# One decode step with its gradients on one core: weight and gradient transfers moved from POOL's DMA queue to ScalarE's ring

## The chip, the cores and the metric

The kernel runs on one core of a Trainium2 chip. The time is device microseconds (us) of one execution; several executions of the unchanged kernel were timed, and one more was recorded by the hardware profiler. PE is the matrix engine, DVE the vector engine, ACT (ScalarE) the activation engine, POOL (GpSimd) the general one, SP (SyncE) an engine that here only issues transfers. A transfer (DMA) is issued by an instruction in an engine's in-order queue and carried by the core's 16 DMA engines.

## The reference

A gated mix of two branches for one token of width 640, and the gradients of everything but one input:

```python
x = A_x                                            # 1 x 1 x 640, bf16
g = sigmoid((x * gate_w).sum(-1))
q = (x @ wq) as 32 heads of 128                    # wq 640 x 4096
p = softmax(q . k_cache * 128**-0.5)               # k_cache, v_cache: 32 x 4096 x 128
a = (p . v_cache) @ wo                             # wo 4096 x 640
h = B_x @ w1 + b1                                  # w1 640 x 1728
b = (h * tanh(softplus(h))) @ w2                   # w2 1728 x 640
out = g * a + (1 - g) * b
# and, for grad_out: d A_x, d k_cache, d v_cache, d wq, d wo, d w1, d b1, d w2, d gate_w
```

Each of K, V, dK and dV is 32 MiB, so 128 MiB of the traffic belong to the caches and their gradients.

## The kernel before, in words

Work goes head by head (32 heads, `h`), in groups of four (`g`, eight groups; `hh` is the head's place in its group). The order of all instructions is written out by hand.

One head: PE transposes V in four blocks (`v_tr`, L448) and ACT copies each block out (L449); the softmax of the head's scores is finished meanwhile (`softmax`: `mx`, `negM`, `e_bf`). DVE makes the previous head's dK (`dk_out`, L511, tile `o_sb`), and SP stores it (L524). `dP` multiplies by the transposed V; the next head's K is transposed and copied (`k_tr`); `probs` finishes p and ds; `dv_out` makes dV. Then `scores(h + 1)` (L454, whose maxima end in ACT's `dgm`, L476), and `dq_o` (L534), the products with V and K themselves. After that SP issues the loads of K for head h + 4 and V for head h + 3: K has four buffers, V three, and `o_sb` four.

Between these steps the code puts the work by groups. For the next group (g + 1): `g_do` (DVE, reads wo) in the third and fourth heads, `g_qcol` (reads wq) in the third, `g_q` in the fourth. For the previous group (g − 1): the gradient of x through wq (`f_dx`), and the gradients of wq and wo, which are written over the weights in place: `f_dwq` on DVE (L317), `f_dwo` on ACT (L323), then the stores `f_dwq_st` (L320) and `f_dwo_st` (L326). A group's wq is 640 rows of 1,024 bytes and its wo 512 rows of 1,280 bytes, 640 KiB each; each has three buffers.

Loads of these weights (`load_wq` L116, `load_wo` L120): group 0 from POOL's queue at the start, groups 1 and 2 from SP's, and the others from POOL's, in the second head of the group two before, after that head's stores. All stores of them are in POOL's queue.

The MLP's work is handed out in small steps in every head from the third on (`mlp_some`, `dw2_some`). Its hidden row is computed in five pieces on one partition, copied to SBUF by ACT (L348) and spread over partitions by five small transfers (L350, L352); two row buffers take turns. Its gradients dw1 and dw2 are written over w1 and w2; their stores stand at L703 to L706, in head 28 of 0 to 31.

The last head is written out after the loop, with the last group's gradients in parts and the small rows of the outputs at the end (L773 to L775). The framework adds the waits on semaphores; an engine runs its own list in order, whatever the others do.

Of the kernel before, what the change touches and what calls it, by code (L numbers as in the profile page):

```python
# [16 lines left out]
def kernel(  # L17
# [24 lines left out]
    nc = tc.nc  # L42
    P = 128
    _, H, Sk, Dh = A_k_cache.shape
    D = A_x.shape[-1]
    F = B_w1.shape[1]
    assert Dh == P and Sk == 32 * P and D % P == 0 and H % 4 == 0 and H >= 16
    J = Sk // P
    RC = D // P
    G = 4  # L50
    NG = H // G
    GD = G * Dh
    FR = F // P
    FM = FR * P
    FT = F - FM
    FCN = FR + 1
# [14 lines left out]
    dwq_v = out_4.rearrange("(rc r) c -> r rc c", r=P)  # L71
    wo_v = A_wo.rearrange("(h d) n -> d h n", d=P)
    dwo_v = out_5.rearrange("(h d) n -> d h n", d=P)
    w1_v = B_w1.rearrange("(rc r) f -> r rc f", r=P)
    dw1_v = out_6.rearrange("(rc r) f -> r rc f", r=P)
    w2_v = B_w2[0:FM, :].rearrange("(p fc) n -> p fc n", p=P)
    dw2_v = out_8[0:FM, :].rearrange("(p fc) n -> p fc n", p=P)
    b1_v = B_b1[0:FM].rearrange("(p fc) -> p fc", p=P)
    b1_t = B_b1[FM:F].rearrange("(p o) -> p o", o=1)
# [6 lines left out]
    out1_rows = out_1.rearrange("a b (c p) -> (a b c) p", p=P)  # L86
# [15 lines left out]
    kts, vts, wqs, wos = {}, {}, {}, {}  # L102
# [6 lines left out]
    def load_v(h):  # L109
        if h < H:  # L110
            vts[h] = kv_in.tile([P, J, Dh], BF16, name="Vn", tag="Vn", bufs=VBUFS)
            nc.sync.dma_start(vts[h][:], Vv[h])

    def load_wq(g, eng):
        wqs[g] = wts.tile([P, RC, GD], BF16, name="wq_g", tag="wq_g")
        eng.dma_start(wqs[g][:], wq_v[:, :, g * GD:(g + 1) * GD])  # L116

    def load_wo(g, eng):
        wos[g] = wts.tile([P, G, D], BF16, name="wo_g", tag="wo_g")
        eng.dma_start(wos[g][:], wo_v[:, g * G:(g + 1) * G, :])  # L120
# [7 lines left out]
    kts[0] = kv_in.tile([P, J, Dh], BF16, name="Kn", tag="Kn")  # L128
    for c in range(2):
        nc.sync.dma_start(kts[0][:, c * JH:(c + 1) * JH, :], Kv[0][:, c * JH:(c + 1) * JH, :])  # L130
    load_wq(0, nc.gpsimd)
    load_wo(0, nc.gpsimd)
    load_v(0)
    load_k(1)
    load_v(1)
# [5 lines left out]
    w1_sb = const.tile([P, RC, F], BF16, name="w1_sb")  # L141
    nc.sync.dma_start(w1_sb[:], w1_v)
    w2_sb = const.tile([P, FCN, D], BF16, name="w2_sb")
# [2 lines left out]
    nc.sync.dma_start(w2_sb[0:FT, FR, :], B_w2[FM:F, :])  # L146
    b1_sb = const.tile([P, FCN], BF16, name="b1_sb")
    nc.vector.memset(b1_sb[:], 0.0)
    nc.gpsimd.dma_start(b1_sb[:, 0:FR], b1_v)
    nc.gpsimd.dma_start(b1_sb[0:FT, FR:FCN], b1_t)  # L150

    ident_bf = const.tile([P, P], BF16, name="ident_bf")
    nc.gpsimd.memset(ident_bf[:], 0.0)
# [10 lines left out]
    def grp(shape, dt, name):  # L164
        return grp_ps.tile(shape, dt, name=name, tag="grp")
# [72 lines left out]
    def g_dobc(g):  # L238
        g_bcast(groups[g]["do_diag"], groups[g]["do_row"], 0, G)
# [11 lines left out]
    def f_bc(g, a=0, b=G):  # L251
        g_bcast(groups[g]["dq_diag"], groups[g]["dq_bc"], a, b)

    def f_aT_pe(g, a=0, b=G):
        gp = groups[g]
        gp["aT_ps"] = grp([P, RC], F32, "aT_ps")
        for c in range(RC):
            for hh in range(a, b):
                nc.tensor.matmul(gp["aT_ps"][:, c:c + 1], lhsT=wos[g][:, hh, c * P:(c + 1) * P],
                                 rhs=gp["o_bf"][:, hh:hh + 1], start=(hh == a), stop=(hh == b - 1))  # L260
# [56 lines left out]
        nc.vector.tensor_scalar(wqs[g][:, c, cs], groups[g]["dq_bc"][:, cs], x_col_f[:, c:c + 1], None, ALU.mult)  # L317

    def f_dwq_st(g):
        nc.gpsimd.dma_start(dwq_v[:, :, g * GD:(g + 1) * GD], wqs.pop(g)[:])  # L320

    def f_dwo(g, hh):
        nc.scalar.activation(wos[g][:, hh, :], da_bc[:], ACT.Copy, scale=groups[g]["dqo"][:, 1, hh:hh + 1])  # L323

    def f_dwo_st(g, a=0, b=G):
        nc.gpsimd.dma_start(dwo_v[:, g * G + a:g * G + b, :], wos[g][:, a:b, :])  # L326

    h_sb = const.tile([P, FCN], F32, name="h_sb")
    u_sb = const.tile([P, FCN], F32, name="u_sb")
# [11 lines left out]
    def m_h(i):  # L341
        n = FW if i < 4 else FT
        ps = grp([1, FW], F32, "h_ps")
        for rc in range(RC):
            nc.tensor.matmul(ps[:, 0:n], lhsT=x_col_bf[:, rc:rc + 1], rhs=w1_sb[:, rc, i * FW:i * FW + n],
                             start=(rc == 0), stop=(rc == RC - 1))
        row = dh_bc[0:1, :].bitcast(F32)[:, (i % 2) * FW:(i % 2) * FW + n]
        nc.scalar.copy(row, ps[:, 0:n])  # L348
        if i < 4:
            nc.gpsimd.dma_start(h_sb[i * P // 4:(i + 1) * P // 4, 0:FR], row)  # L350
        else:
            nc.gpsimd.dma_start(h_sb[0:FT, FR:FCN], row)  # L352

    def m_np(fc):
        return P if fc < FR else FT
# [107 lines left out]
    def v_tr(h, c):  # L463
        if c == 0:
            VT[h] = kvT.tile([P, J, P], BF16, name="VT", tag="VT")
        tr_block(vts[h], VT[h], c)
# [11 lines left out]
    def softmax(h):  # L478
        mx = s_ps.tile([P, P + 2], F32, name="mx", tag="mx")
        nc.tensor.matmul(mx[:, 0:P], lhsT=scale_f[:], rhs=dgms.pop(h)[:], start=True, stop=True)  # L480
        negM = small.tile([P, 1], F32, name="negM", tag="negM")
        nc.vector.tensor_reduce(negM[:], mx[:, 0:P], axis=AX.X, op=ALU.max, negate=True)  # L482
        es[h] = small.tile([P, J], BF16, name="e_bf", tag="e_bf")
        zds[h] = small.tile([P, 2], F32, name="zd", tag="zd")
        nc.scalar.activation(es[h][:], S_ps.pop(h)[:], ACT.Exp, bias=negM[:], scale=scale, accum_out=zds[h][:, 0:1])  # L485
        return mx

    def dP(h):
        DP_ps[h] = s_ps.tile([P, J], F32, name="DP", tag="DP")
        cols_mm(DP_ps[h][:], VT.pop(h), doz[h // G % 2][:, h % G, :])  # L490
        pj = small.tile([P, J], F32, name="pj", tag="pj")
        nc.vector.scalar_tensor_tensor(pj[:], in0=DP_ps[h][:], scalar=1.0, in1=es[h][:],
                                       op0=ALU.mult, op1=ALU.mult, accum_out=zds[h][:, 1:2])
# [32 lines left out]
    def dv_out(h):  # L526
        out_pair(h, dVv, p4s[h], groups[h // G]["do_row"])

    def dk_out(h):
        out_pair(h, dKv, ds4s[h], groups[h // G]["qs_row"])  # L530
# [92 lines left out]
    for h in range(H - 1):  # L623
        g, hh = h // G, h % G
        nx, pv = g + 1 < NG, g > 0
        v_tr(h, 0)
        v_tr(h, 1)
        mx = softmax(h)
        if h > 0:
            dk_out(h - 1)  # L630
        if hh == 0 and pv:
            g_dobc(g)
        v_tr(h, 2)
        v_tr(h, 3)
        dP(h)
        if hh == 0 and pv:
            f_bc(g - 1)
            f_aT_pe(g - 1)
        k_tr(h + 1, 0)
        k_tr(h + 1, 1)  # L640
        zd_mm(h, mx)
        if hh == 0 and pv:
            f_dx(g - 1, 0)
        if hh == 1 and pv:
            f_dx(g - 1, 3)
        if hh == 2 and nx:
            g_do(g + 1, 0)
        if hh == 3 and nx:
            g_do(g + 1, 3)
        probs(h, mx)  # L650
        k_tr(h + 1, 2)
        k_tr(h + 1, 3)
        dv_out(h)
        scores(h + 1)
        od = dq_o(h)
        load_k(h + KBUFS)
        load_v(h + VBUFS)
        dqo_red(h, od)
        budget = 0.0
        if hh == 0:  # L660
            if nx:
                g_new(g + 1)
            if pv:
                f_aT_add(g - 1)
                f_dx(g - 1, 1)
                f_dx(g - 1, 2)
                f_dwo(g - 1, 0)
                f_dwo(g - 1, 1)
            budget = 2.7
        if hh == 1:  # L670
            if pv:
                f_dx(g - 1, 4)
                for c in range(RC):
                    f_dwq(g - 1, c)
                f_dwq_st(g - 1)
                f_dwo(g - 1, 2)
                f_dwo(g - 1, 3)
                f_dwo_st(g - 1)
            if g + 2 < NG:
                load_wq(g + 2, nc.gpsimd if pv else nc.sync)  # L680
                load_wo(g + 2, nc.gpsimd if pv else nc.sync)
            budget = 1.8
        if hh == 2:
            if nx:
                g_do(g + 1, 1)
                g_do(g + 1, 2)
                g_qcol(g + 1)
            budget = 2.7
        if hh == 3:
            if nx:  # L690
                g_docol(g + 1)
                g_dodiag(g + 1)
                g_q(g + 1)
                g_qs(g + 1)
                f_new(g)
                f_diag(g)
            budget = 1.8
        if h >= 2:
            mlp_some(budget)
            dw2_some(2)  # L700
        if h == H - 4:
            assert not mq and dw2_next[0] == FCN
            nc.gpsimd.dma_start(dw1_v, w1_sb[:])  # L703
            for a, b in W2P:
                nc.gpsimd.dma_start(dw2_v[:, a:b, :], w2_sb[:, a:b, :])
            nc.gpsimd.dma_start(out_8[FM:F, :], w2_sb[0:FT, FR, :])  # L706
            nc.sync.dma_start(db1_row, dh_bc[0:1, :])

    g, h = NG - 1, H - 1
# [61 lines left out]
    fin_rows = const.tile([3 * RC, P], BF16, name="fin_rows")  # L771
    nc.scalar.copy(fin_rows[:], fin_ps[:])
    nc.scalar.dma_start(out0_rows, fin_rows[0:RC, :])  # L773
    nc.gpsimd.dma_start(out1_rows, fin_rows[RC:2 * RC, :])
    nc.scalar.dma_start(out9_rows, fin_rows[2 * RC:3 * RC, :])  # L775
    dk_out(h)

# [29 lines left out]
```

## Time and profile before

| | |
|---|---|
| median of 3 runs | 418.42 us (418.15 to 419.58) |
| profiled execution | 420.13 us, its span 418.4 us |
| busy PE, DVE, ACT, POOL | 320.5, 303.1, 216.3, 38.1 us |
| moved by DMA | 165.05 MB, mean 395 GB/s |
| of that in SP's and in POOL's queue | 141.28 MB and 22.79 MB |
| mean granted TensorE clock | 0.893 |

The span is the time from the first to the last instruction. In the profile's list of slices each digit is a fortieth of the span, busy share in tenths. In its DMA part, q1 is the hardware ring that SP uses, q10 the one that ACT uses, and q0 the queue that POOL feeds by software. A wait is told as the line that waited and what it waited for, with the total, the number of times and the longest. DMA share is the mean busy share of the 16 engines; it can read slightly over 1.

### The profile page before, as it was taken

How to read it: one execution, taken by the hardware profiler on the slowest of the kernel's cores; microseconds unless marked ns; L12 is line 12 of the kernel's file. 1: busy time of each engine (PE TensorE's matmuls, PEld its weight loads, DVE VectorE, ACT ScalarE, POOL GpSimd, SP SyncE). 2: the span in 40 equal slices, each digit the busy share in tenths (PEclk: the TensorE clock that was granted, in tenths of full speed). 3: DMA queues.
4: the chain of work that ended last, by engine and by line, in shares of the span. 5: the costliest groups of instructions: out<-in, count | busy, mean ns of one | idle time of the engine just before them, and what ended most of it. 6: DMA issues, size and time to landing. Idle time of an engine off the chain costs nothing.

```text
span 418.4 us, 15402 instructions
## 1 busy us (share of the span) xinstructions
PE 320.5 (77%) x6797; PEld 291.5 (70%) x6797; DVE 303.1 (72%) x816; ACT 216.3 (52%) x447; POOL 38.1 (9%) x61
## 2 busy tenths in 40 slices
PE   1598959888699779777987889777897888847850
PEld 1487838777679778767877778666787787747740
DVE  0536645787868987798869796888887987718681
ACT  2255434674346635455666764665445644545560
POOL 5000010001100100001104100001000040000120
PEclk9999898999789998888998898878988989959985
DMA  8999999999999999999999999999999999999956
GB/s 292 394 408 422 420 397 418 417 378 412 404 406 356 387 417 405 414 411 404 410 389 420 424 418 408 421 415 352 407 385 423 383 418 420 416 421 415 401 228 244
DMA packets 28074, 165.05 MB, mean 395 GB/s; under 512 B 3093, under 2 KB 5462, under 8 KB 12007
## 3 DMA queue, kind: packets, MB, share of 16 engines
q1 hardware_dynamic: 22402, 141.28, 83.7%
q0 software_dynamic: 5552, 22.79, 13.8%
q8 instruction: 53, 0.87, 0.8%
q14 instruction: 15, 0.11, 0.1%
q10 hardware_dynamic: 52, 0.01, 0.0%
HBM read 82.03 MB, written 82.03 MB: 392 GB/s over the span
## 4 chain that ended last, share of the span: by engine, by line
PE 39%; ACT 22%; DVE 20%; DMA 11%; issue 5%; DVEq 0%; POOL 0%; ACTq 0%; POOLq 0%
PE tr L448 16%; PE od L534 11%; ACT VT L449 8%; ACT KT L449 7%; DMA out_dram<-o_sb 6%; DVE o_sb L511 4%; DMA wo_g<-in_A_wo_dram 3%; PE S L454 3%; PE DP L454 3%; DVE junk L408 2%; PE q_ps L197 2%; DVE junk L219 2%; DVE junk L270 2%; DVE mjunk L430 2%; ACT e_bf L485 2%
## 5 line engine op out<-in xcount | busy, mean ns | idle before, releaser
L448 PE MATMUL tr<-ident_bf,Vn 128*128 128x128 bf16 x1024 | 78.8, 236 | 24.7 <-ACT VT L449 15.5
L449 ACT COPY KT<-tr 128x512 f32<-128x512 f32 x128 | 70.5, 587 | 48.7 <-PE tr L448 48.6
L448 PEld LDWEIGHTS <-Vn 128*128 128x128 bf16 x1024 | 70.4, 107 | 35.4 <-issue 25.3
L448 PE MATMUL tr<-ident_bf,Kn 128*128 128x128 bf16 x1024 | 83.5, 245 | 6.9 <-DMA Kn<-in_A_k_cache_dram 5.0
L448 PEld LDWEIGHTS <-Kn 128*128 128x128 bf16 x1024 | 76.9, 114 | 8.8 <-DMA Kn<-in_A_k_cache_dram 4.9
L449 ACT COPY VT<-tr 128x512 f32<-128x512 f32 x128 | 69.4, 586 | 23.4 <-PE tr L448 22.8
L511 DVE TENSOR_TENSOR o_sb<-qs_row,ds 128x2048 bf16<-128x2048 bf16 x64 | 78.1, 1263 | 2.9 <-DMA out_dram<-o_sb 2.9
L511 DVE TENSOR_TENSOR o_sb<-do_row,p 128x2048 bf16<-128x2048 bf16 x64 | 75.2, 1217 | 1.1 <-DMA out_dram<-o_sb 1.1
L454 PE MATMUL DP<-doz,VT 128*128 128x32 bf16 x1024 | 39.6, 179 | 27.9 <-ACT VT L449 24.1
L454 PEld LDWEIGHTS <-VT 128*128 128x128 bf16 x1024 | 33.2, 98 | 32.9 <-ACT VT L449 31.8
L454 PE MATMUL S<-qz,KT 128*128 128x32 bf16 x1024 | 36.9, 180 | 3.1 <-ACT KT L449 0.4
L476 ACT ACTIVATE dgm<-ident_bf,m 128x128 f32<-128x128 bf16 x32 | 12.9, 402 | 50.3 <-DVE m L474 50.3
L454 PEld LDWEIGHTS <-KT 128*128 128x128 bf16 x1024 | 32.4, 98 | 6.4 <-ACT KT L449 5.8
L534 PE MATMUL od<-p,Vn 128*128 128x32 bf16 x1024 | 31.5, 177 | 3.9 <-issue 3.9
L534 PE MATMUL od<-ds,Kn 128*128 128x32 bf16 x1024 | 31.2, 177 | 2.3 <-issue 2.3
L534 PEld LDWEIGHTS <-Vn 128*128 128x128 bf16 x1024 | 28.4, 96 | 4.4 <-issue 4.4
L534 PEld LDWEIGHTS <-Kn 128*128 128x128 bf16 x1024 | 28.3, 96 | 2.6 <-issue 2.6
L270 DVE SCALAR_TENSOR_TENSOR junk<-wq_g,dq_bc 128x512 bf16<-128x512 bf16 x35 | 23.5, 687 | 4.0 <-ACT dq_bc L233 4.0
L320 POOL DMA_DIRECT2D out_dram<-wq_g x8 | 7.1, 886 | 206.6 <-DVE wq_g L317 108.0
L219 DVE SCALAR_TENSOR_TENSOR junk<-wo_g,da_bc 128x640 bf16<-128x640 bf16 x32 | 25.5, 820 | 0.4 <-DMA wo_g<-in_A_wo_dram 0.4
L482 DVE TENSOR_REDUCE negM<-mx 128x1 f32<-128x128 f32 x32 | 9.2, 288 | 22.8 <-PE mx L480 22.7
L323 ACT ACTIVATE wo_g<-da_bc,dqo 128x640 bf16<-128x640 bf16 x32 | 24.5, 813 | 0.0
(157 smaller groups left out, 326.8 us busy)
## 6 DMA issues: line engine op xcount, KB each, us to landing
out_dram<-o_sb SPq DMA_DIRECT2D x62, 1024.0 KB, 10.4
Vn<-in_A_v_cache_dram SPq DMA_DIRECT2D x32, 1024.0 KB, 14.8
Kn<-in_A_k_cache_dram SPq DMA_DIRECT2D x31, 1024.0 KB, 15.5
out_dram<-wq_g POOLq DMA_DIRECT2D x8, 640.0 KB, 10.5
out_dram<-wo_g POOLq DMA_DIRECT2D x7, 640.0 KB, 14.2
wq_g<-in_A_wq_dram POOLq DMA_DIRECT2D x6, 640.0 KB, 11.7
wo_g<-in_A_wo_dram POOLq DMA_DIRECT2D x6, 640.0 KB, 12.1
w_sb<-in_B_w_dram SPq DMA_DIRECT2D x1, 2160.0 KB
```

The source lines that it names most:

```text
L197: nc.tensor.matmul(ps[:], lhsT=x_col_bf[:, rc:rc + 1].to_broadcast([P, P]), rhs=wqs[g][:, rc, :], start=(rc == 0), stop=(rc == RC - 1))
L219: nc.vector.scalar_tensor_tensor(junk[:], in0=wos[g][:, hh, :], scalar=1.0, in1=da_bc[:], op0=ALU.mult, op1=ALU.mult, accum_out=gp["do_col ...
L270: nc.vector.scalar_tensor_tensor(junk[:, cs], in0=wqs[g][:, c, cs], scalar=1.0, in1=gp["dq_bc"][:, cs], op0=ALU.mult, op1=ALU.mult, accum_ ...
L323: nc.scalar.activation(wos[g][:, hh, :], da_bc[:], ACT.Copy, scale=groups[g]["dqo"][:, 1, hh:hh + 1])
L408: nc.vector.scalar_tensor_tensor(junk[0:n, :], in0=w2_sb[0:n, fc, :], scalar=dm[0:n, fc:fc + 1], in1=db_bc[0:n, :], op0=ALU.mult, op1=ALU. ...
L448: nc.tensor.transpose(tp[:, t, :], src[:, c * TB + t, :], ident_bf[:])
L449: nc.scalar.copy(dst[:, sl, :].rearrange("p a b -> p (a b)").bitcast(F32), tp[:].rearrange("p a b -> p (a b)").bitcast(F32))
L454: nc.tensor.matmul(out, lhsT=T[:, j, :], rhs=zrow[:, J - 1 - j:2 * J - 1 - j], start=(j == 0), stop=(j == J - 1))
L476: nc.scalar.activation(dgms[h][:], ident_bf[:], ACT.Copy, scale=m32[:])
L482: nc.vector.tensor_reduce(negM[:], mx[:, 0:P], axis=AX.X, op=ALU.max, negate=True)
L511: nc.vector.tensor_tensor(dst[:, a:b, :].rearrange("p j (k t) -> p j k t", t=4), row.rearrange("p (k t) -> p k t", t=4).unsqueeze(1).to_br ...
L534: nc.tensor.matmul(out, lhsT=N[:, j, :], rhs=c4[:, 4 * j:4 * j + W], start=(j == 0), stop=(j == J - 1))
```

## The change

- Group 0's wq and wo are loaded from SP's queue, wq after the first half of head 0's K, wo after its second half.
- The other loads of wq and wo from group 2 on, all stores of their gradients but one, the two pieces of b1, the hidden row's five transfers, the stores of dw1 and dw2 and one output row are issued by ScalarE. The store of the last group's wq gradient is issued by SP.
- The weights of group g + 1 are loaded at the end of the first head of group g (from g = 1 on), where before those of g + 2 were loaded in the second head of g.
- The store of a group's wq gradient stands one head later, in the third head of the next group.

```diff
     for c in range(2):
         nc.sync.dma_start(kts[0][:, c * JH:(c + 1) * JH, :], Kv[0][:, c * JH:(c + 1) * JH, :])
-    load_wq(0, nc.gpsimd)
-    load_wo(0, nc.gpsimd)
+        (load_wo if c else load_wq)(0, nc.sync)
...
-    nc.gpsimd.dma_start(b1_sb[:, 0:FR], b1_v)
-    nc.gpsimd.dma_start(b1_sb[0:FT, FR:FCN], b1_t)
+    nc.scalar.dma_start(b1_sb[:, 0:FR], b1_v)
+    nc.scalar.dma_start(b1_sb[0:FT, FR:FCN], b1_t)
...
     def f_dwq_st(g):
-        nc.gpsimd.dma_start(dwq_v[:, :, g * GD:(g + 1) * GD], wqs.pop(g)[:])
+        (nc.sync if g == NG - 1 else nc.scalar).dma_start(dwq_v[:, :, g * GD:(g + 1) * GD], wqs.pop(g)[:])
...
     def f_dwo_st(g, a=0, b=G):
-        nc.gpsimd.dma_start(dwo_v[:, g * G + a:g * G + b, :], wos[g][:, a:b, :])
+        nc.scalar.dma_start(dwo_v[:, g * G + a:g * G + b, :], wos[g][:, a:b, :])
...
         if i < 4:
-            nc.gpsimd.dma_start(h_sb[i * P // 4:(i + 1) * P // 4, 0:FR], row)
+            nc.scalar.dma_start(h_sb[i * P // 4:(i + 1) * P // 4, 0:FR], row)
         else:
-            nc.gpsimd.dma_start(h_sb[0:FT, FR:FCN], row)
+            nc.scalar.dma_start(h_sb[0:FT, FR:FCN], row)
...
         if hh == 0:
+            if nx and pv:
+                load_wq(g + 1, nc.scalar)
+                load_wo(g + 1, nc.scalar)
             if nx:
                 g_new(g + 1)
...
                     f_dwq(g - 1, c)
-                f_dwq_st(g - 1)
                 f_dwo(g - 1, 2)
                 f_dwo(g - 1, 3)
                 f_dwo_st(g - 1)
-            if g + 2 < NG:
-                load_wq(g + 2, nc.gpsimd if pv else nc.sync)
-                load_wo(g + 2, nc.gpsimd if pv else nc.sync)
             budget = 1.8
         if hh == 2:
+            if pv:
+                f_dwq_st(g - 1)
...
         if h == H - 4:
             assert not mq and dw2_next[0] == FCN
-            nc.gpsimd.dma_start(dw1_v, w1_sb[:])
+            nc.scalar.dma_start(dw1_v, w1_sb[:])
             for a, b in W2P:
-                nc.gpsimd.dma_start(dw2_v[:, a:b, :], w2_sb[:, a:b, :])
-            nc.gpsimd.dma_start(out_8[FM:F, :], w2_sb[0:FT, FR, :])
+                nc.scalar.dma_start(dw2_v[:, a:b, :], w2_sb[:, a:b, :])
+            nc.scalar.dma_start(out_8[FM:F, :], w2_sb[0:FT, FR, :])
...
-    nc.gpsimd.dma_start(out1_rows, fin_rows[RC:2 * RC, :])
+    nc.scalar.dma_start(out1_rows, fin_rows[RC:2 * RC, :])
```

## The prediction

> **What bounds the kernel now.** I read the page first, its slices and DMA queues above all.
>
> ```profile
> PE 320.5 (77%) x6797; PEld 291.5 (70%) x6797; DVE 303.1 (72%) x816; ACT 216.3 (52%) x447; POOL 38.1 (9%) x61
> DMA  8999999999999999999999999999999999999956
> DMA packets 28074, 165.05 MB, mean 395 GB/s; under 512 B 3093, under 2 KB 5462, under 8 KB 12007
> q1 hardware_dynamic: 22402, 141.28, 83.7%
> q0 software_dynamic: 5552, 22.79, 13.8%
> PE 39%; ACT 22%; DVE 20%; DMA 11%; issue 5%; DVEq 0%; POOL 0%; ACTq 0%; POOLq 0%
> ```
>
> No engine is over 77%, POOL is not on the chain of waits, and the 16 DMA engines are full until some 20 us before the end. Two limits lie close together: a relay of PE, ACT and DVE of 11.9 us a head (a group's q_ps, the last of its four heads, starts at 69.6 and at 354.5 us, six groups apart: 285/24), and the DMA. A group moves 16 MiB of K, V and their gradients and 2.5 MiB of weights and theirs, 19.4 MB in 47.5 us, 408 GB/s. The stretches (columns: PE, PEld, DVE, ACT, POOL busy, clock, DMA share, GB/s) show how near that is to the most the DMA does:
>
> ```profile
> 18.00:24.00 6.00, 3.67 (x17) 1.99 (x17) 2.57 (x11) 1.64 (x4) 0.00 (x0) 1.00 1.05 381
> 54.00:60.00 6.00, 3.19 (x28) 1.93 (x28) 2.50 (x6) 0.87 (x2) 1.04 (x2) 1.00 1.06 388
> 150.00:156.00 6.00, 4.78 (x128) 4.39 (x124) 4.98 (x13) 1.48 (x3) 0.86 (x1) 1.00 1.02 420
> 366.00:372.00 6.00, 0.00 (x0) 0.00 (x0) 1.50 (x8) 1.84 (x3) 0.00 (x0) 0.54 1.02 421
> 396.00:402.00 6.00, 5.29 (x154) 4.90 (x152) 3.54 (x10) 4.62 (x9) 0.00 (x0) 1.00 0.36 145
> ```
>
> In the fourth row PE does nothing for 6 us: V of head 29 is late. In the last the DMA is two thirds idle, since the last heads' outputs are not made yet. The timelines and the waits say why:
>
> ```profile
> 336.89 0.86 POOL L703 DMA_DIRECT2D out_dram<-w_sb  x1
> 366.48 1.53 ACT L323 ACTIVATE wo_g<-da_bc,dqo 128x640 bf16<-128x640 bf16 x2
> 372.06 1.89 PE L448 MATMUL tr<-ident_bf,Vn 128*128 128x128 bf16 x16 [6.63 <-DMA Vn<-in_A_v_cache_dram]
> ...
> 11.95 0.69 PE L209 MATMUL qc_ps<-cols_bf,wq_g 128*128 128x1 bf16 x20 [4.99 <-DMA wq_g<-in_A_wq_dram]
> ...
> SPq L120 <- DMA vec_rows<-in_gate_w_dram: 0.4, 1, 0.4
> SPq L707 <- DMA Vn<-in_A_v_cache_dram: 3.6, 1, 3.6
> ```
>
> The 4.4 MB of dw1 and dw2, written in the code at head 28, leave at 337 us, during head 25: POOL has nothing else in its queue and runs ahead. They hold up V29. The last two rows show SP holding a transfer for an unrelated one. The instruction records name the reason: SP's and ScalarE's transfers take turns on the same eight completion semaphores, and one is issued when the earlier holder of its semaphore has landed. POOL's have eight of their own.
>
> **The change part by part**, against the profiled execution (420.13 us, span 418.4); the median, 418.42, is 1.7 lower, and I carry differences over to it.
>
> *Start.* wq and wo of group 0 shared the engines with K0, V0, K1; wq landed at 11.9 us, wo about 15.5 to 16.2. On SP between the halves of K0, wq has only 0.52 MB ahead of it: from the first bytes at 2.3 us, 1.18 MB at some 360 GB/s (GB/s is 227 to 400 over 2 to 8 us) is 5.6 us, and 1 us or so to land: 7.0. Likewise wo 9.7. From wq to the first g_do took 4.4 us, so head 0 starts 4.9 us earlier. V0 and K1, now behind 1.31 MB more, land near 11.5 and 14 and are used from 18 and 22. Cover: the prefetch; without it the gain shrinks to nothing. Bounds −4.9 to 0; I take −4.9. The two b1 transfers go onto ScalarE's ring ahead of its first copy (6.0 us), two issues of 0.3 us: hidden, unless rival 3 holds.
>
> *Issue time.* On SP a wq transfer took 0.43 us to issue, wo 0.38 (the second wo's 3.64 us was SP's ring full with 1,800 rows; ScalarE's has at most 1,152 of weights). ScalarE gets, in each of groups 1 to 6: wq and wo in the group's first head (0.81), dwo in its second (0.38), dwq in its third (0.43). In first heads, ScalarE today goes from dgm through two f_dwo (1.53) straight into the V copies, 0.9 to 1.1 us from dgm's end: nothing hides the 0.81. In second heads likewise, with f_dwo_st behind the last f_dwo. In third heads it waits 1.0 to 2.2 us there with nothing to do: 0.43 hidden. So 1.2 us × 6 = 7.2 us in the way of the copies. The chain runs through f_dwo in three of seven groups, which makes 3.1 us the floor; I take 5.1. The five h_sb transfers move with their 5 us landing (L348 waits 4.4 for one): nothing, ±2. POOL's own 0.86 and 0.77 us issues were on no chain: nothing.
>
> *Packets.* The page's counts tell how each ring cuts the rows. 2,369 packets lie between 512 B and 2 KB, and SP's two wq, two wo and the tail of w2 have 2,368 rows of 1,024 and 1,280 B: a hardware ring moves row by row. POOL's 14 wq-shaped and 14 wo-shaped transfers alone are 16,128 rows in 5,552 packets: joined by four. The packet records give 46 ns for 1,024 B, 58 for 1,280, and 159 for 4,096, 196 for 5,120. Per pair, (640 × (46 − 159/4) + 512 × (58 − 196/4))/16 = 0.54 us. The first two stretches above, with such pairs, lose (418−381)/418 × 6 = 0.53 and 0.43 us. Twelve pairs before head 28's end: 6.5 us, if stores cost what loads do (none is in the trace on a hardware ring: from 0 to 10). Against that stands that 3.5 MB of dw1 and dw2 no longer pass by then, 8.4 us at 415 GB/s. So the DMA has 1.9 us less to do by that point, and I take 0, with +6.5 as the bound, if heads 1 to 24 are held by the DMA.
>
> A rule speaks differently here: in the Trainium skill, DMA: Bandwidth & Descriptors, section Specifications, transfers reach line rate from 512 B; these rows would then cost nothing extra, and the sum would be the same with a bound of 0. The 46 ns row decides. The same page (Issuing engines are not separate DMA queues) says that all issuers use the same engines and that only issue time is saved; by that rule the move off POOL brings nothing at all.
>
> *Weights one group ahead.* They are issued at the end of a group's first head and wanted by g_do in its third, some 20 us on; such pairs on POOL's ring landed in 10 to 14 us (counting its completion packets). Covered by 6 us; nothing. Without cover DVE waits, some 2 us a group.
>
> *Tail.* f_dwo of head 28 ends at 368.0 us; then ScalarE issues dw1, dw2 (three) and the remainder: 5 × 0.44 = 2.2. V29 is in time now, so its copies start at 370.2, not 373.19: −3.0. But the eight semaphores: the fifth of the burst needs V30 landed, the fourth K31, issued at 352.9 to 356.2 us. Landings of V took 10 to 17 us with no dw stores about, so V30 lands at 366 to 374: a wait of 0 to 6 us with the copies of V29 queued behind it on ScalarE, PE behind them; I take 3. From there 46 us of relay remain, and the DMA has 17.5 MB left: 42.2 us at 415 GB/s and 1.1 for two pairs. It fits, so the idle stretch fills at no gain. Last, dwq of group 7 goes ahead of SP's last outputs and more transfers share the eight semaphores: 0 to 2, I take 1.
>
> *Mid-run waits.* dwo's issue needs K of the head before landed: 12 us after that issue; K landed after 9 to 14, and the new weight loads add up to 1.31 MB/410 = 3.2. So between none and 5 us; over six groups I take 1 us in all, the before's landings at those places (9.2, 8.9, 7.4) being the nearest.
>
> Sum: −4.9 + 5.1 + 0 − 3.0 + 3 + 1 + 1 = +2.2. From 418.42: 420.6 us.
>
> **The rivals.**
> 1. *Faster, 412.5 us.* ScalarE's issues fall into its 48% idle time (L449 waits 48.6 us for PE). Then the start's −4.9, the tail's −3.0 and +2 for the end remain: −5.9. For it: the chain gives ACT only 22%. Against it: the places of the issues have no slack. It cannot go much lower: the same bytes and 7.5 us of packets fit only because about 5 us of idle DMA at 396 to 408 get filled. Chance 0.30.
> 2. *Slower, 429 us: the shared semaphores.* ScalarE, in order, stands at dwo_st (and at load_wo) until an SP transfer eight places back has landed. Price: a mean overshoot of 2 us × 6 groups where the sum has 1 in all, and 5 instead of 3 in the tail: +13, less about 4 that the idle DMA near the end gives back, on top of 420.6. It decides once K loads take over 12 us in second heads. For it: late V loads of 14 to 17 us; against it, the 7.4 to 9.2 above. Chance 0.20.
> 3. *b1 on ScalarE waits for a load eight places earlier.* V2 landed at 26.7 us; the copies would start 10 us later and the start's gain be lost: about 427. The first eight semaphores seem to go round in the order of issue, so b1 would be early. Held within rival 2's chance.
> 4. *No change, 418.4:* the start and ScalarE's issues cancel, the tail too. Chance 0.14.
>
> **How the numbers follow.** The forecast (0.36) spreads ±3 about 420.6. About 0.3%, 1.26 us, is what can be told from no change. Below 417.2: most of rival 1, a little of the forecast and of 4: 0.33. Within: 0.18. Above 419.7: 0.26 of the forecast, rival 2, a little of 4: 0.49. The range runs from rival 1's value to rival 2's, 412 to 429.
>
> **What would show it.** Right: q0 gone; some 16,000 packets under 2 KB; qc_ps at 7 us; ScalarE's copies after dgm 0.8 us later in first heads; dw1 leaving at about 368; no PE wait for V29; stretches with weights at 380 to 390 GB/s. Rival 2: ScalarE's queue waiting for Kn or Vn; DMA shares under 0.9 mid-run. Wrong: stores whose 1 KB rows take far more or less than 50 ns, or weights that DVE waits for.

## The result, and the profile after

The changed kernel takes 440.24 us (median of 4 runs, 437.77 to 444.15); the kernel before, on the same chip, 419.0. The ratio is 1.0515 [1.0433, 1.0598], so it is 21 us slower, and outside the predicted range of 412 to 429. The profiled execution took 437.77 us, its span 435.8. Ratios below have their 95% intervals, and "us against before" is the ratio's excess times 419.

The page after: engines, slices, queues and the chain of waits.

```profile
PE 321.1 (74%) x6789; PEld 292.7 (67%) x6797; DVE 301.2 (69%) x816; ACT 217.4 (50%) x447; POOL 6.0 (1%) x19
DMA  8999998999999999989999999999999999998877
DMA packets 40786, 165.05 MB, mean 379 GB/s; under 512 B 3342, under 2 KB 21903, under 8 KB 24720
q1 hardware_dynamic: 23058, 141.93, 82.3%
q10 hardware_dynamic: 17662, 22.14, 14.2%
DMA 31%; PE 23%; DVE 15%; ACT 14%; issue 3%; ACTq 1%; DVEq 0%; SPq 0%
```

The engines do the same work as before, but the DMA's part of the chain has gone from 11% to 31%. POOL's queue is gone, and 16,441 packets more lie under 2 KB, as the count of rows said. The row of slices hides the loss: a slice is 10.9 us, and nearly every digit is still 9. Stretches of 6 us show it (columns: busy time of PE, PEld, DVE, ACT, POOL with instructions, clock, DMA share, GB/s):

```profile
72.00:78.00 6.00, 5.86 (x164) 5.57 (x165) 4.25 (x12) 3.14 (x6) 0.00 (x0) 1.00 0.77 283
186.00:192.00 6.00, 5.20 (x131) 4.92 (x130) 4.93 (x13) 4.08 (x7) 0.00 (x0) 0.80 0.76 284
384.00:390.00 6.00, 0.00 (x0) 0.00 (x0) 0.00 (x0) 0.00 (x0) 0.00 (x0) 0.50 1.01 424
408.00:414.00 6.00, 5.78 (x155) 5.58 (x154) 4.08 (x13) 2.70 (x7) 0.00 (x0) 1.00 0.73 280
420.00:426.00 6.00, 2.64 (x72) 2.31 (x68) 4.71 (x20) 4.28 (x10) 0.00 (x0) 0.82 0.70 268
```

In the first two stretches the 16 DMA engines are a quarter idle while PE computes: SP has just stood, or stands, at a store and issues nothing (11.1 us until 72.7 for a transfer of the hidden row, 18.4 us until 190.2 for a load of wq). Near the end there is the opposite, 6 us in which no engine computes and the DMA is full. Over the whole span idleness is the smaller part of the loss: the packets' times, added up and divided by 16, are 424.4 us where they were 411.7 before, so of the 17.4 us by which the span grew 4.7 are idle DMA and 12.7 longer packet time, 6.4 of it in the shorter rows and 6.2 in the packets of 8 KB, 327.6 ns each against 321.4. What the issuing engines did, first SP's queue by its waits (total us, times, longest):

```profile
SPq L523 <- DMA wq_g<-in_A_wq_dram: 83.6, 5, 19.1
SPq L112 <- DMA out_dram<-wq_g: 43.3, 4, 14.8
SPq L112 <- DMA out_dram<-wo_g: 23.3, 2, 14.9
SPq L107 <- DMA wq_g<-in_A_wq_dram: 15.1, 1, 15.1
SPq L523 <- DVE m L473: 8.6, 5, 4.3
```

L523 stores dK and dV, L107 and L112 load K and V: none has anything to do with wq or wo. Before, what L524 (now L523) waited for longest was DVE, which makes what it stores:

```profile
SPq L524 <- DVE m L474: 134.2, 30, 8.4
```

Now SP stands for weights. One such stand, in SP's and ScalarE's timelines and in the chain of waits (start us, us, what):

```profile
123.34 17.54 SPq L523 DMA_DIRECT2D out_dram<-o_sb  x2
140.97 0.40 SPq L107 DMA_DIRECT2D Kn<-in_A_k_cache_dram  x1
142.27 0.71 SPq L112 DMA_DIRECT2D Vn<-in_A_v_cache_dram  x1
```
```profile
126.92 0.39 ACTq L116 DMA_DIRECT2D wq_g<-in_A_wq_dram  x1
127.40 0.68 ACTq L120 DMA_DIRECT2D wo_g<-in_A_wo_dram  x1
```
```profile
127.40 14.81 DMA wo_g<-in_A_wo_dram
142.27 10.04 DMA Vn<-in_A_v_cache_dram
152.35 1.89 PE tr L447 x16
```

SP reaches the second of two stores at 123.7 us. Its semaphore's earlier holder is a wq load that ScalarE has not even issued: ScalarE comes to it at 126.92, when its own program gets there. The load lands at about 140.5, 13.6 us after its issue; only then does SP go on to K, and to V when the wo load behind it has landed too (142.2), and PE waits for that V until 152.35. The tail has the same the other way round, in ScalarE's timeline (in brackets: idle time and what ended it):

```profile
372.69 0.38 ACTq L703 DMA_DIRECT2D out_dram<-w_sb  x1
374.00 1.53 ACTq L705 DMA_DIRECT2D out_dram<-w_sb  x2
393.70 0.56 ACTq L706 DMA_DIRECT2D out_dram<-w_sb  x1
394.36 1.07 ACT L448 COPY VT<-tr 128x512 f32<-128x512 f32 x2 [19.84 <-DMA out_dram<-w_sb]
```

The fifth and smallest of the dw stores, 80 KB, stands 18 us until dw1, issued 21 us earlier, has landed: the instruction records give both the same semaphore. The copies of V of head 29 stand behind it, and PE behind them, for 18.1 us:

```profile
395.00 1.23 PE L447 MATMUL tr<-ident_bf,Vn 128*128 128x128 bf16 x10 [18.12 <-ACT VT L448]
```

### The profile page after: what moved, and what is told of

It is laid out like the page before. It is cut to its first block, busy times and chain, and to the rows that moved or that the text cites. A ratio compares the mean times of both kernels' runs of the same rounds, so it can differ in the third digit from the quotient of the medians.

```text
span 435.8 us, 15353 instructions
## 1 busy us (share of the span) xinstructions
PE 321.1 (74%) x6789; PEld 292.7 (67%) x6797; DVE 301.2 (69%) x816; ACT 217.4 (50%) x447; POOL 6.0 (1%) x19
## 4 chain that ended last, share of the span: by engine, by line
DMA 31%; PE 23%; DVE 15%; ACT 14%; issue 3%; ACTq 1%; DVEq 0%; SPq 0%
DMA Vn<-in_A_v_cache_dram 12%; PE tr L447 11%; DMA wo_g<-in_A_wo_dram 7%; DVE o_sb L510 7%; DMA out_dram<-o_sb 6%; ACT VT L448 6%; DMA out_dram<-w_sb 5%; PE od L533 4%; ACT KT L448 3%; PE DP L453 2%; ACT wo_g L322 2%; PE q_ps L196 1%; DMA h_sb<-dh_bc 1%; ACT e_bf L484 1%; DVE junk L407 1%
## 5 line engine op out<-in xcount | busy, mean ns | idle before, releaser
L447 PE MATMUL tr<-ident_bf,Vn 128*128 128x128 bf16 x1024 | 83.3, 245 | 62.1 <-ACT VT L448 40.6
L447 PEld LDWEIGHTS <-Vn 128*128 128x128 bf16 x1024 | 74.8, 111 | 74.0 <-issue 45.8
L447 PE MATMUL tr<-ident_bf,Kn 128*128 128x128 bf16 x1024 | 79.6, 238 | 7.7 <-DMA Kn<-in_A_k_cache_dram 5.8
L510 DVE TENSOR_TENSOR o_sb<-qs_row,ds 128x2048 bf16<-128x2048 bf16 x64 | 75.3, 1219 | 7.3 <-DMA out_dram<-o_sb 7.2
L447 PEld LDWEIGHTS <-Kn 128*128 128x128 bf16 x1024 | 73.7, 111 | 9.8 <-DMA Kn<-in_A_k_cache_dram 5.7
L453 PEld LDWEIGHTS <-VT 128*128 128x128 bf16 x1024 | 33.5, 99 | 19.8 <-ACT VT L448 18.3
L533 PEld LDWEIGHTS <-Vn 128*128 128x128 bf16 x1024 | 28.3, 96 | 3.4 <-issue 3.4
L533 PEld LDWEIGHTS <-Kn 128*128 128x128 bf16 x1024 | 28.1, 96 | 0.8 <-issue 0.8
L491 DVE SCALAR_TENSOR_TENSOR pj<-DP,e_bf 128x32 f32<-128x32 f32 x32 | 6.0, 189 | 30.1 <-PE DP L453 29.6
## 6 DMA issues: line engine op xcount, KB each, us to landing
out_dram<-wq_g ACTq DMA_DIRECT2D x7, 640.0 KB, 18.1
wq_g<-in_A_wq_dram ACTq DMA_DIRECT2D x6, 640.0 KB, 12.7
```

What stands on the lines that cost most here:

```text
L447: nc.tensor.transpose(tp[:, t, :], src[:, c * TB + t, :], ident_bf[:])
L453: nc.tensor.matmul(out, lhsT=T[:, j, :], rhs=zrow[:, J - 1 - j:2 * J - 1 - j], start=(j == 0), stop=(j == J - 1))
L510: nc.vector.tensor_tensor(dst[:, a:b, :].rearrange("p j (k t) -> p j k t", t=4), row.rearrange("p (k t) -> p k t", t=4).unsqueeze(1).to_br ...
L533: nc.tensor.matmul(out, lhsT=N[:, j, :], rhs=c4[:, 4 * j:4 * j + W], start=(j == 0), stop=(j == J - 1))
```

## The experiments

Two theories. **T** (tail): the 18 to 20 us at 393.7 are the wait of the last dw store on dw1's semaphore. **S** (shared semaphores, mid-run): SP is held at semaphores whose earlier holder is a transfer of ScalarE that was issued late, or only just now, and has not landed. Their rival, **R** (rows): weights cut into rows of 1,024 and 1,280 bytes cost the DMA engines more. Others come up on the way: ScalarE's issue time, the number of transfers that share the semaphores, the large stores themselves.

**The five dw stores back on POOL (e1), and those alone on ScalarE (e2).**

```diff
-            nc.scalar.dma_start(dw1_v, w1_sb[:])
+            nc.gpsimd.dma_start(dw1_v, w1_sb[:])   # e1: after, with dw2's four parts likewise
...
-            nc.gpsimd.dma_start(dw1_v, w1_sb[:])
+            nc.scalar.dma_start(dw1_v, w1_sb[:])   # e2: before, with dw2's four parts likewise
```

> The changed kernel with the five stores of dw1 and dw2 back in POOL's queue, all else as changed. Theory T (ScalarE stands 20 us at the last of these stores, for dw1's own landing on the shared semaphore): that wait goes, V29 is late again by some 5 us, so 440 - 20 + 5 = 425, range 420 to 428. Theory S (the time is lost mid-run, where SP's outputs and loads of V wait for weight transfers on the shared semaphores): little changes, 434 to 440.

> The kernel before with only the five stores of dw1 and dw2 on ScalarE. T: the last of the five waits for dw1 to land, some 18 us, less the 6.6 us for V29 that are no longer there: 419 + 12 = 431, range 427 to 437. S: 419 to 422, as the weights' transfers stay on POOL's own semaphores.

e1 took 434.22 us, ratio 1.0336 [1.0278, 1.0394], 6.0 less than the change; e2 426.71, 1.0184 [1.0128, 1.0241], 7.7 against before. In e2 the stall is there in a kernel that is otherwise the one before:

```profile
ACT VT L449 <- DMA out_dram<-w_sb: 18.2, 1, 18.2
```

So the tail costs 6 to 8 us of its 18 to 20, and some two thirds of the loss are elsewhere. That the rest of the 18 is made up because the DMA works on meanwhile (share 1.01 at 384 to 390) is argued and not shown.

**The weights back on POOL (e3), and the start alone (e4).**

```diff
-                load_wq(g + 1, nc.scalar)
-                load_wo(g + 1, nc.scalar)
+                load_wq(g + 1, nc.gpsimd)               # e3: after, dwq and dwo stores on gpsimd too
+                load_wo(g + 1, nc.gpsimd)
...
-    load_wq(0, nc.gpsimd)
-    load_wo(0, nc.gpsimd)
+        (load_wo if c else load_wq)(0, nc.sync)         # e4: before, with this only
```

> The changed kernel with all loads of wq and wo from group 2 on, and all stores of their gradients, back in POOL's queue, at the places in the code that the change gave them; dw1, dw2, b1 and the hidden row stay on ScalarE. T: the stall of ScalarE in the tail stays, 431 to 438. S: the mid-run loss goes, 420 to 425.

> The kernel before with only group 0's weights on SP, between the halves of K0. Head 0 starts 4.5 us earlier. If the relay sets the pace up to head 28: 414 to 416. If the DMA does: 418 to 419.

e3 took 427.18, 1.018 [1.0135, 1.0225], between the ranges of the two theories: what is left is about e2's cost, with a `VT` wait of 19.8 us. The weights on ScalarE, their shorter rows included, are thus worth 13 us. e4 took 418.29, 0.9977 [0.995, 1.0004]. The start does come earlier (the same copy of V's transpose in the first head is at 19.06 us in e4, at 19.64 in the changed kernel and at 23.94 before), and almost nothing of it is left at the end.

**Loads alone (e7) and stores alone (e8) on ScalarE**, both from e1:

```diff
-        nc.scalar.dma_start(dwo_v[:, g * G + a:g * G + b, :], wos[g][:, a:b, :])
+        nc.gpsimd.dma_start(dwo_v[:, g * G + a:g * G + b, :], wos[g][:, a:b, :])   # e7, dwq too
...
-                load_wq(g + 1, nc.scalar)                                          # e8, wo too
+                load_wq(g + 2, nc.gpsimd if pv else nc.sync)   # in the second head, as before
```

> The kernel of e1_dw_pool with the stores of the weights' gradients back on POOL; the loads stay on ScalarE, one group ahead. S: the longest holds, SP's outputs for the loads of wq, stay: 428 to 431. P: half of the short rows: 419 + 3 = 422. Start gain included in both.

> The kernel of e1_dw_pool with the loads of the weights back on POOL at the places and two groups ahead as before; the stores of their gradients stay on ScalarE. S: the holds of V's loads for the stores stay, 423 to 426. P: 422.

e7: 427.9, 1.0195 [1.0156, 1.0235]; e8: 431.4, 1.0265 [1.0227, 1.0303]. In each SP waits longest, in total, for a transfer that ScalarE issued shortly before; e7's line first, then e8's:

```profile
SPq L107 <- DMA wq_g<-in_A_wq_dram: 86.2, 6, 16.3
```
```profile
SPq L112 <- DMA out_dram<-wo_g: 89.7, 6, 16.3
```

Half of the transfers hold SP for as long as all do at one line. The costs, 8 and 11 us, don't add up to e1's 14, and the stores cost more than was expected of them (423 to 426).

**Long rows (e5 from e1, e6 from before).** The weights and their gradients are moved as 128 rows of 5,120 bytes, so their elements are in another order and the values are not the reference's.

```diff
-    wq_v = A_wq.rearrange("(rc r) c -> r rc c", r=P)
+    wq_v = A_wq.rearrange("r c -> (r c)").rearrange("(g p a c) -> g p a c", g=NG, p=P, a=RC)
```

> The kernel of e1_dw_pool (changed, but dw1 and dw2 on POOL), with the weights and their gradients moved in rows of 5,120 B per partition: the same bytes from and to the same tensors, their elements in another order, so the values are not the reference's. Theory P (rows of 1 KB, one packet each on a hardware ring, cost DMA time): 434 - 6.4 = 427.5, range 426 to 429. Theory S (SP is held for the weights' landings on the shared semaphores, the DMA queue runs short): 431 to 434, the landings being only a little earlier.

> The kernel before with the same rows of 5,120 B. POOL's queue joins the short rows by four already (4,096 B in 159 ns, 5,120 in 196), so both theories: no change, 418 to 419.5; the two pairs on SP's ring at the start give at most 1 us.

e5: 422.3, 1.0057 [1.0029, 1.0085], 12 us less than e1 and below the ranges of both theories; e6: 415.4, 0.989 [0.9851, 0.9928], 4.6 less than before, where none was expected. Rows do cost: in e6 the packets of 8 KB took 2.4 us less of the 16 engines than before and all others 3.4 less (86.5 against 89.9). But e5 says less for R than it seems: SP's waits shrink with the rows, since the transfers that hold it land sooner (e1's lines, then e5's):

```profile
SPq L523 <- DMA wq_g<-in_A_wq_dram: 88.8, 5, 23.2
SPq L112 <- DMA out_dram<-wq_g: 54.5, 4, 15.2
```
```profile
SPq L523 <- DMA wq_g<-in_A_wq_dram: 62.0, 5, 14.7
SPq L112 <- DMA out_dram<-wq_g: 15.9, 4, 5.8
```

**The same short rows on SP's ring (e10)**, which parts R from S: rows, places and bytes are e1's, but SP issues the transfers (the last group's dwo stays on ScalarE).

```diff
-                load_wq(g + 1, nc.scalar)
-                load_wo(g + 1, nc.scalar)
+                load_wq(g + 1, nc.sync)                  # the stores too
+                load_wo(g + 1, nc.sync)
```

> The kernel of e1_dw_pool with the weights' loads and gradient stores on SP's ring instead of ScalarE's (the last group's dwo stays on ScalarE), at the same places. Short rows as on ScalarE, but one ring in order, so that a semaphore's earlier holder has always been sent before. S (a slow second ring holds SP): the holds and the idle DMA go, the rows stay: 425 to 428. P alone: 432 to 435, as on ScalarE.

421.97 us, 1.0072 [1.0037, 1.0106]: 3.0 against before, and 12.3 less than e1 (below the range of either theory), with as many short packets:

```profile
DMA packets 40418, 165.05 MB, mean 395 GB/s; under 512 B 3342, under 2 KB 21839, under 8 KB 24352
```

So R is worth 3 us here, with whatever the start gives taken off, and the two issuers 12. Weights held SP for 224 us in e1 and for 8 in e10. How the holds become 12 us is shown only in part: e1's profiled span is 16.8 us longer than e10's (434.8 against 418.0), with 6.0 us more of idle DMA (11.1 against 5.1) and 10.5 us more in the 8 KB packets, 328 ns each against 317.5. Short rows moving beside them are not what slows these: in e1 the 8 KB packets that overlapped a row of 1,280 bytes or less took 322 ns, the others 334. What does was not tried.

**24 transfers of 1.2 KB (e9)**: before, with four small loads a group in groups 1 to 6 at the places where the change issues weights; then what they consist of, apart.

```diff
+    def tiny():
+        t = small.tile([RC, P], BF16, name="tiny", tag="tiny", bufs=4)
+        nc.scalar.dma_start(t[:], gw_rows)              # e12: nc.sync, e13: nc.gpsimd
...
+        if pv and nx:
+            for _ in range((2, 1, 1, 0)[hh]):
+                tiny()       # e11: in its place nc.scalar.copy of ident_bf into a 128x128 tile
```

> The kernel before with 24 added loads of 1.2 KB on ScalarE, into tiles that nobody reads, four in each of groups 1 to 6 where the changed kernel has its weight transfers. They take as many of the shared semaphores and as many issues of ScalarE (0.3 us each, 7 us in all), but move nothing. If the number of holders or ScalarE's issue time is what costs: 426 to 432. If it is how long the weights take to land on ScalarE's ring, or their rows: 419 to 421.

> Before, with 24 extra copies of a 128x128 tile on ScalarE at the places of e9's tiny transfers; no transfer is added. A copy of that size takes 0.39 us in the trace of before, e9's issues 0.26 to 0.50 each. If ScalarE's issue time is what cost e9 its 7 us: 424 to 427 us (24 x 0.39 = 9.4 us as the most). If it is the semaphores that SP shares with ScalarE: within 2 us of before, and no wait of SP for anything new.

> Before, with e9's 24 tiny transfers at the same places in the code, issued by SP in place of ScalarE. As many transfers share the eight semaphores, but SP alone issues them in the order in which they take turns. If the number of holders is the cost: 424 to 427 us. If it is that SP must wait for ScalarE to come to its place in its program: 417 to 420 us, and SP's waits for tiny below 20 us in all (e9: 103 us at three lines).

> Before, with e9's 24 tiny transfers issued by POOL, whose semaphores SP does not use. Both theories of e9, ScalarE's time and the shared semaphores, expect no change: 417.5 to 419.5 us, and no wait of SP for tiny. If the transfers themselves disturb the DMA engines: as slow as e9, 425 us.

| | issued by | us | against before |
|---|---|---|---|
| e9 | ScalarE | 425.84 | 1.0181 [1.0132, 1.0231] |
| e11 | ScalarE, copies and no transfers | 418.67 | 0.9978 [0.9952, 1.0004] |
| e12 | SP | 419.28 | 1.0012 [0.9977, 1.0047] |
| e13 | POOL | 420.43 | 1.0026 [0.9998, 1.0053] |

Transfers of 31 KB in all cost 7.6 us if ScalarE issues them, and nothing that can be told if SP or POOL does. It is not ScalarE's time either: e11's copies took 0.285 us each, as much as e9's issues (0.26), at the same places (a weight's issue, 0.4 to 1.2 us, was not copied in length). Nor is it the number of holders of the semaphores, which is the same in e12. What is left is that two engines with programs of their own take turns at the semaphores. e9's SP queue, then e12's only line with `tiny`:

```profile
SPq L528 <- DMA tiny<-in_gate_w_dram: 48.7, 6, 9.8
SPq L107 <- DMA tiny<-in_gate_w_dram: 28.8, 8, 5.1
SPq L112 <- DMA tiny<-in_gate_w_dram: 25.5, 6, 4.8
```
```profile
SPq L107 <- DMA tiny<-in_gate_w_dram: 0.3, 1, 0.3
```

103 us of SP's time become 0.3, which settles S for these loads. In e9 a load of 1.2 KB has SP wait up to 9.8 us: SP stands at a store from 123.5 to 133.3, and ScalarE reaches the load at 128.99. In this hold, the longest, 5.5 us pass before the issue, but that is not the rule. Of the 103 us only 22 lie before ScalarE has issued the load and 81 after that, the load landing 4 to 6.5 us behind its issue; of the 183 us for which weights hold SP in the kernel after, 12 lie before the issue and 171 after it (a wq load lands after 12 to 19 us). In those of over 10 us ScalarE issued from 7 us before to 5 after SP came to its turn, so most of the landing falls on SP; where SP issues everything, the earlier holder has landed by then.

**The last dw store alone (e14 from after, e15 from e2)** goes to POOL:

```diff
-            nc.scalar.dma_start(out_8[FM:F, :], w2_sb[0:FT, FR, :])
+            nc.gpsimd.dma_start(out_8[FM:F, :], w2_sb[0:FT, FR, :])
```

> After, with only the last of the five dw stores (the remainder of dw2) on POOL, so that no transfer stands behind dw1 on ScalarE's queue at head 29. If the wait of that small store is what the tail lost: ScalarE's 19.8 us wait ahead of the V copies is under 5 us, and the time is that of e1, 432 to 436 us. If the 4.3 MB on ScalarE's ring hold up V30 whoever waits: 438 to 442 us, with PE waiting 10 us or more for Vn.

> Before, with dw1 and the three large stores of dw2 on ScalarE, and the small last one on POOL. The same two theories: 418 to 421 us where the small store's wait was the whole cost of e2 (426.7), 425 to 428 us where the large ones are.

e15: 419.59, 1.0012 [0.9978, 1.0045]. The whole cost of e2 was that one transfer of 80 KB; the 4.3 MB before it cost nothing on ScalarE, though their issues keep ScalarE to 370.72 us. T holds in the kernel before. In the changed kernel it can't be told from the time: e14 took 436.38, 1.0384 [1.0317, 1.0451], 3.9 less than the change and 2.2 more than e1, and its interval overlaps both. Its trace shows that the wait moves on, to SP and to the next store on ScalarE (lines of SP's timeline, then of ScalarE's):

```profile
382.46 15.75 SPq L523 DMA_DIRECT2D out_dram<-o_sb  x2
398.31 0.71 SPq L112 DMA_DIRECT2D Vn<-in_A_v_cache_dram  x1
```
```profile
400.99 0.39 ACTq L325 DMA_DIRECT2D out_dram<-wo_g  x1
401.42 1.07 ACT L448 COPY VT<-tr 128x512 f32<-128x512 f32 x2 [7.65 <-DMA out_dram<-w_sb]
```

**A way ahead? (c1, c2).** All weights on POOL, and dw2 stored one head later in POOL's order (dw1 stays); c2 adds the start.

```diff
-                load_wq(g + 2, nc.gpsimd if pv else nc.sync)
+                load_wq(g + 2, nc.gpsimd)                # wo, and group 1 at the start, likewise
...
+        if h == H - 3:                                   # dw2's stores, from H - 4
```

> The kernel before with the two pairs of weights that SP loaded (groups 1 and 2) on POOL, joined by four there, and with the stores of dw2 behind head 29's stores in POOL's queue, so that they leave at about 387 us instead of 338. DMA work falls by 1.1 us, V29 is not late, and 2.2 MB fill the idle DMA at 396 to 402 us: if the DMA sets the pace, 419 - 1 - 4 = 414, range 413 to 417; if the relay does, 418 to 420.

> c1_pool_late with group 0's weights on SP between the halves of K0, as in the change. The relay starts 4.5 us earlier, one pair goes in short rows (0.5 us). If the DMA sets the pace: equal to c1 within 1 us. If the relay does by now: 3 to 4 us below c1.

418.08, 0.9991 [0.9962, 1.002], and 419.5, 1.0019 [0.999, 1.0049]: no gain. V29's stall of before, 6.63 us, is 2.68 in c1 and gone in e15 (where a later V is 4.28 late), and neither is faster: it costs nothing in the end, with the DMA full through it (1.02 at 366 to 372). e4's 0.9977 is no better founded, since e11, which only adds work, reads 0.9978. No version here with the reference's values was shown to beat the kernel before.

## Why the prediction was wrong

The loss parts as follows, by medians: the change less e1, 6.0 us (dw stores); e1 less e10, 12.3 (weights issued by ScalarE in place of SP); e10 less before, 3.0 (rows, start, and the small moves). The intervals of the ratios leave about 4, 3 and 1.4 us of doubt on them.

- **Mid-run waits, taken as 1 us: 12.** This is the step that failed. It asked when ScalarE's stores would wait for SP's transfers, and found their landings short enough. The other direction was missing: SP's stores and loads wait for ScalarE's transfers, 183 us in all in the kernel after, most of it landing time. With the weights issued by SP (e10) 12.3 us of the loss are gone. "It decides once K loads take over 12 us in second heads" was the wrong condition: e9 leaves the weights where they were, adds 31 KB, and costs 7.6 us.
- **Rival 2** named the shared semaphores, and its mid-run shares of DMA under 0.9 came (0.76 and 0.77), but it expected "ScalarE's queue waiting for Kn or Vn". Its price, 13 us less about 4 above the forecast, was half of what the two semaphore terms came to (12.3 and 6.0).
- **Tail, −3.0 and +3: +6 for −3 + 3.** The mechanism, the fifth store of the burst holding the copies of V29, was right; its holder was not V30 ("a wait of 0 to 6 us") but dw1, the first of the same burst, and the wait 18. Eight semaphores do not mean that the last eight transfers hold them: the records of the kernel after give dw1 and the fifth store the same one. V29 was 2.1 us late instead of 6.6, nearly as forecast, but that is worth nothing: c1 and e15 shorten or remove its lateness and stay at 0.9991 and 1.0012.
- **Start, −4.9: −1.0 [−2.1, +0.2] (e4).** The 4.9 us in the first head came in e4 as forecast, and are not seen at the end; that the full DMA takes them back fits c1 and e6, but was not shown by itself.
- **ScalarE's issue time, +5.1: none (e11, −0.9 [−2.0, +0.2]).** Copies as long as e9's issues, at the same places, cost nothing, so rival 1 was right on this term: "the places of the issues have no slack" is true head by head and did not matter in the end, though a load of wo took 0.7 to 1.25 us to issue on ScalarE and not 0.38.
- **Packets, 0 with +6.5 as the bound.** The term itself was well sized: rows of 1,024 and 1,280 bytes took 61.0 us of the 16 engines after, and the same weights 54.6 before, 6.4 more. The offset against it, the 8.4 us of dw1 and dw2 stored later, was not one. Of the 6.4, e10 shows 3.0 at the end, less whatever the start gives.
- **The hidden row's transfers, "nothing, ±2".** They held SP too, 20.9 us in the profiled run. What that cost in the end was not told apart; e3, which keeps them, is 0.5 us above e2.
- **b1 (rival 3)** held up nothing: `qc_ps` began at 8.02 us, forecast 7.

Issue time and start were both costed on the relay; neither measured anything, while e6, with 5.8 us less of packet time in its profile, is 4.6 us faster. So the DMA's work, not the relay, bound the kernel before.

The Trainium skill, DMA: Bandwidth & Descriptors, section Specifications, has rows from 512 bytes at line rate. The runs differ: in the kernel after 1,024 bytes took 47.5 ns and 5,120 bytes 199, so five short rows take 238. e6, with longer rows for the same bytes, is 1.1% faster, though most of the rows it lengthens were joined by four before. Its section Issuing engines are not separate DMA queues says that issuing from several engines only saves issue time. As to bandwidth the runs agree, since two issuers (e1) moved no more than one (e10), 380 GB/s against 395; as to time the choice of the issuing engine was worth 12 us, in a framework that has two of these engines take turns on semaphores.

## What to carry to other kernels

Before moving a transfer to another queue, list which transfers share its completion semaphore, and in which engine's program each stands: a queue that runs far ahead (here SP, loading K and V) must not take turns with one that issues between its computations. Keep a ring's prefetches in one issuer, or put strangers on a queue with semaphores of its own. And read DMA idleness in stretches shorter than a slice, next to the waits of the issuing queue itself.

## What the runs showed that was not expected

- A transfer of 1.2 KB can cost 0.3 us on average (7.6/24) with no bytes to speak of, by which engine issues it.
- Packets of one size do not always take the same time: the 8 KB packets of the V loads took 332 ns on average before, 351 after, and 321 in e10; at 222 to 225 us of the kernel after those that started took 554. Over 16,020 packets on 16 engines, e1's 328 for all of them against e10's 317.5 are 10.5 us of DMA work. Why was not tried.
